# A list scheduler for the attention and gate stage of a fused transformer block, and the low part of the attention output taken from TensorE

## The chip, the cores and the metric

The kernel runs on one core of one Trainium2 chip. The metric is the device time of one execution in microseconds; lower is better. The core has five engines with a queue each: TensorE (PE, matmuls), VectorE (DVE), ScalarE (ACT), GpSimd (POOL) and SyncE (SP, which issues most DMAs). Each engine works off its own queue, in which its instructions stand in the program's order.

## The reference

`x` is the output of attention inside chunks of 64 rows (batch 8, 8 heads, 576 rows, head size 64). It goes through a gate, a projection and a feed-forward net:

```python
scores = scale * np.matmul(q_c, k_c.transpose(0, 1, 2, 4, 3))
scores = scores - np.max(scores, axis=-1, keepdims=True)
attn = np.exp(scores)
attn = attn / (np.sum(attn, axis=-1, keepdims=True) + 1e-09)
out = np.matmul(attn, v_c)
...
for k in range(K):
    gate_pre += conv_w[k][None, None, :] * xp[:, k:k + S, :]
gate = 1.0 / (1.0 + np.exp(-gate_pre))
val = x @ w_val
return (gate * val @ w_out).astype(np.float32)
...
ch = np.maximum(xn @ w_ch1, 0.0) @ w_ch2
return (x + ch).astype(np.float32)
```

The convolution has 5 taps, the model width is 512, the hidden width 2048, `xn` is a layer norm. Products keep float32 accuracy by splitting each operand into a high part (`F32R`) and a low part (operand minus high part): high·high, high·low and low·high are summed. The weights of the projections arrive as 64-bit numbers and are decoded on the chip to float32.

## The kernel before, in words

The 4608 rows of all batches are worked in 9 blocks of 512 rows (`NB`), and attention in 18 units of 256 rows (`NU`), two to a block.

For a unit u: `load_qkv` (line 78) fetches q, k and v. `a3` (line 152) makes the scores (S: 32 small matmuls, two records each in the trace), and the softmax on DVE in five steps (maximum line 167, subtract 170, sum 176, reciprocal 177, multiply 179) with the exponential on ACT (174). `a4` (181) turns the weights on PE (T: 8 transposes) and copies them out with ACT (pT, 188). `a5` (208) multiplies them with v (A: 32 small matmuls into the PSUM tile `x`, of which there is one) and takes three things out of PSUM: the float32 output `xf` (ACT, 233), its high part `xh` (ACT, 236) and its low part `xl` (DVE, 238: `x` minus `xh`).

For a block j: `conv` (243) computes the gate's sum in `cg`, the first tap on ACT (248), four more on DVE (250) for each of four column groups f, 16 operations of 128x516 to a block (in the first and last block 32 of 128x256 or a little more). `sigm` (255) is one sigmoid on ACT. `val` (266, called V here) is 12 matmuls of 512 columns for each f, into a PSUM ring `ps_d` of two buffers; its result is multiplied with the gate on DVE (`gv`, 282), and split by ACT (`gh`, 285) and DVE (`gl`, 286). A buffer of `ps_d` comes free with `gv`, which needs the sigmoid. `proj` (289, called O) is 12 matmuls for each of four row tiles, copied out by ACT (`y`, 299) and sent to DRAM. The multiplications of `chain` all have line 264.

The weights are decoded and split in between (`split`, 92): ACT (87), three DVE operations (88 to 90), ACT (95), and the low part on POOL (96). `early_ff` does so for the first 4 of 16 pairs of feed-forward weights.

What sets the order: `slot` (594) calls these functions by a table (`at`, lines 656 to 679). For the first four slots PE's order is the program's (`manual_schedule`); WARM adds dummy matmuls. From then on, and on all other engines throughout, the framework's scheduler sets the order by priority, which follows the program's order except under `high_priority`. After the last attention unit `prep` (623) starts the layer norm and the transposes (`turn_rows`, 343) for block 0 of the feed-forward stage, which then runs in its own order (lines 713 to 764) to the end.

Of the kernel before, what the change touches and what calls it, by code (L numbers as in the profile page):

```python
# [8 lines left out]
F32 = mybir.dt.float32  # L9
# [6 lines left out]
DRAM = bass.MemoryType.DRAM  # L16


@with_exitstack
def tile_chunk_attention_gated_mlp(ctx: ExitStack, tc: tile.TileContext, qk, v, w_val, conv_w, w_out, g_ln, w1, w2, out):  # L20
# [52 lines left out]
    gr = const.tile([CT, P], F32, name="gr")  # L73

# [23 lines left out]

    wv = {}

    def load_w(w, nm, slot0):
        raws = []
        for c in range(CT):
            raw = wA.tile([P, DM, 2], U32, tag=f"s{slot0 + c}", name="raw")
            nc.sync.dma_start(out=raw, in_=w[c * P:(c + 1) * P])
            raws.append(raw)
        wv[nm] = raws

    def split_w(nm, c0=0, c1=CT):
# [40 lines left out]
    pt, pT = {}, {}  # L150

    def a3(u):
        t = qkr.pop(u)
        kt, qt = t[:, 0], t[:, 1]
        sc = ps_s.tile([P, 2, NG, CH], F32, tag="sc", name="sc")
        for g in range(NG):
            n, hp = divmod(g, NP)
            for c in range(2):
                cs = slice(n * P + c * CH, n * P + (c + 1) * CH)
                for par in range(2):  # L160
                    r0 = CH * par
                    nc.tensor.matmul(
                        out=sc[CH * c:CH * c + CH, par, g, :], lhsT=qt[r0:r0 + CH, hp, cs], rhs=kt[r0:r0 + CH, hp, cs],
                        start=True, stop=True,
                    )
        mx = pA.tile([P, 2, NG], F32, tag="mx", name="mx")
        nc.vector.tensor_reduce(out=mx, in_=sc, op=ALU.max, axis=AX.X)  # L167
        whole = exps[u % len(exps)]
        ex = whole[:, :, :, 0:CH]
        nc.vector.tensor_tensor(  # L170
            out=ex.rearrange("p g r k -> p r g k"), in0=sc,
            in1=mx.unsqueeze(3).to_broadcast([P, 2, NG, CH]), op=ALU.subtract,
        )
        nc.scalar.activation(out=ex, in_=ex, func=ACTF.Exp, scale=scale)
        sm = pA.tile([P, NG, 2], F32, tag="sm", name="sm")
        nc.vector.tensor_reduce(out=sm, in_=whole, op=ALU.add, axis=AX.X)  # L176
        nc.vector.reciprocal(out=sm, in_=sm)
        pr = pt[u] = pA.tile([P, NG, 2, CH], F32, tag="pr", name="pr")
        nc.vector.tensor_tensor(out=pr, in0=ex, in1=sm.unsqueeze(3).to_broadcast([P, NG, 2, CH]), op=ALU.mult)

    def a4(u):
        pr = pt.pop(u)
        t = pA.tile([P, NG, P], F32, tag="pT", name="pT", bufs=1)
        ps = ps_p.tile([P, NG, P], F32, tag="p", name="pst")
        for g in range(NG):
            nc.tensor.transpose(out=ps[:, g, :], in_=pr[:, g].rearrange("p r k -> p (r k)"), identity=ident)
        with tc.high_priority():
            nc.scalar.activation(out=t, in_=ps, func=ACTF.Copy)
            pT[u] = t

    xf, xh, xl = {}, {}, {}

    def new_block(j):
        o = boundary(j)
        t = pD2.tile([P, CT, BLK + 2 * HALO], F32, tag="xf", name="xf")
        if j == 0:
            nc.gpsimd.memset(t[:, :, 0:HALO], 0.0)
        else:
            ob = boundary(j - 1)
            e = BLK + (HALO if ob < BLK else 0)  # L200
            nc.gpsimd.tensor_copy(out=t[:, :, 0:HALO], in_=xf[j - 1][:, :, e:e + HALO])
        if o < BLK:
            nc.gpsimd.memset(t[:, :, HALO + o:2 * HALO + o], 0.0)
        xf[j] = t
        xh[j] = pD2.tile([P, CT, BLK], F32R, tag="xh", name="xh")
        xl[j] = pD2.tile([P, CT, BLK], F32R, tag="xl", name="xl")

    def a5(u):
        t = pT.pop(u)
        j, uu = divmod(u, UPB)  # L210
        va = vr.pop(u)
        x = ps_x.tile([P, 2, NP // 2, UN], F32, tag="x", name="x")
        for i in range(NP // 2):
            for c in range(NC):
                n, cs = c // 2, slice(c % 2 * CH, (c % 2 + 1) * CH)
                for f in range(2):
                    for r in range(2):
                        r0, o0 = CH * r, CH * f
# [582 lines left out]
```

## Time and profile before

| what | us |
|---|---|
| median of 3 runs (1138.92 to 1139.91) | 1139.91 |
| span of the profiled execution, first to last instruction | 1134.2 |
| PE busy in the span | 1070.5 (94%) |
| DVE busy | 712.8 (63%) |
| ACT busy | 483.5 (43%) |
| POOL busy | 110.6 (10%) |

For the profiled execution its span is given and no total of its own; the median of the runs lies 5.7 us above the span. The span falls into three parts: the stage that is changed, from 0 to about 344 us, where the first feed-forward matmul starts; a first feed-forward block to about 456; and the rest, in which PE has hardly a gap. Two notes on reading: a row with "x64" merges that many instructions, and the durations of neighbours on one engine overlap a little, so that the step from one start to the next is the price of an instruction in a queue.

### The profile page before, as it was taken

Reading aid. Unit: us, or ns where it says so; the run is one execution under the profiler, and the core shown is the slowest. Engines: PE = TensorE matmul, PEld = TensorE weight load, DVE = VectorE, ACT = ScalarE, POOL = GpSimd, SP = SyncE. Lnnn points to the kernel's source line nnn. Section 1 sums busy time; section 2 is a strip of 40 time slices with the busy share of each in tenths; the row PEclk is TensorE's granted clock in tenths of the full one; section 3 lists DMA queues with packets and bytes.
Section 4 is the critical chain, followed back from the end, with each engine's and each line's share of the span. In section 5 each row is a group of like instructions: output and inputs, shape, how many; then the busy total and the mean of one; then the engine's idle time right before and its main releaser. Section 6 shows DMA issues by size and latency. Waiting matters only on the chain.

```text
span 1134.2 us, 17091 instructions
## 1 busy us (share of the span) xinstructions
PE 1070.5 (94%) x6862; PEld 871.4 (77%) x6862; DVE 712.8 (63%) x1171; ACT 483.5 (43%) x832; POOL 110.6 (10%) x120
## 2 busy tenths in 40 slices
PE   5788989899898989899999999999999999999998
PEld 5676767777786868688888888888888888878877
DVE  6999999888967877545647434447444437432434
ACT  3566666566574754434444123333223333221221
POOL 2021001000003443322210000000000000000000
PEclk9799999999999999999999999999999999999999
DMA  8535546531135753634342733332733222622212
GB/s 334 169 121 166 187 133 213 179 107 72 46 120 188 225 165 119 236 118 145 126 141 100 232 99 106 112 106 89 232 105 103 99 93 89 227 93 93 75 38 75
DMA packets 58581, 155.28 MB, mean 137 GB/s; under 512 B 5742, under 2 KB 13958, under 8 KB 56198
## 3 DMA queue, kind: packets, MB, share of 16 engines
q1 hardware_dynamic: 53318, 144.75, 37.7%
q10 hardware_dynamic: 5184, 9.44, 2.2%
q8 instruction: 54, 0.88, 0.3%
q14 instruction: 25, 0.20, 0.1%
HBM read 116.41 MB, written 37.75 MB: 136 GB/s over the span
## 4 chain that ended last, share of the span: by engine, by line
PE 65%; DVE 24%; issue 4%; ACT 3%; DMA 3%; POOL 0%; SPq 0%; ACTq 0%; POOLq 0%; DVEq 0%
PE acc L499 16%; PE x L525 15%; PE psf L499 14%; PE zy L525 10%; DVE cg L250 7%; PE psv L264 5%; DVE da L89 2%; DVE da L90 2%; DVE sm L176 2%; PE acc L385 1%; DVE xl L238 1%; DMA raw<-in_moe_w_ch 1%; DVE h L537 1%; PE psh L264 1%; DVE mx L167 1%
## 5 line engine op out<-in xcount | busy, mean ns | idle before, releaser
L545 DVE TENSOR_TENSOR c<-x,c 128x512 f32<-128x512 f32 x96 | 66.2, 690 | 237.3 <-ACT c L541 181.1
L499 PE MATMUL psf<-w,h 128*128 128x512 f32 x768 | 186.0, 391 | 0.0
L499 PE MATMUL acc<-w,h 128*128 128x512 f32 x768 | 186.0, 391 | 0.0
L499 PEld LDWEIGHTS acc<-w,h 128*128 128x128 f32 x768 | 144.2, 188 | 31.4
L499 PEld LDWEIGHTS psf<-w,h 128*128 128x128 f32 x768 | 144.2, 188 | 31.4
L525 PE MATMUL x<-t,wc 128*128 128x512 f32 x576 | 148.2, 393 | 3.4 <-DVE c L545 3.4
L541 ACT ACTIVATE c<-zy 128x512 f32<-128x512 f32 x96 | 58.0, 604 | 188.4 <-PE zy L525 188.3
L525 PEld LDWEIGHTS x<-t,wc 128*128 128x128 f32 x576 | 108.8, 189 | 27.8 <-DVE c L545 4.6
L536 ACT ACTIVATE h<-c 128x512 fp32r<-128x512 f32 x96 | 60.5, 631 | 136.1 <-DVE c L545 135.5
L250 DVE SCALAR_TENSOR_TENSOR cg<-xf,cw,cg 128x516 f32<-128x516 f32 (+1 forms) x176 | 108.6, 661 | 0.0
L504 DVE TENSOR_TENSOR yt<-psf,yt 128x512 f32<-128x512 f32 x128 | 88.2, 691 | 25.0 <-PE psf L499 21.1
L525 PE MATMUL zy<-b,wc 128*128 128x512 f32 x384 | 98.9, 393 | 0.0
L525 PEld LDWEIGHTS zy<-b,wc 128*128 128x128 f32 x384 | 71.2, 188 | 14.6
L537 DVE SCALAR_TENSOR_TENSOR h<-c,h 128x512 fp32r<-128x512 f32 x96 | 68.5, 713 | 14.0 <-ACT h L536 13.9
L264 PE MATMUL psv<-xh,vh 128*128 128x512 f32 x144 | 62.1, 432 | 15.5 <-DVE gv L282 15.5
L96 POOL TENSOR_TENSOR w<-da,w 128x512 fp32r<-128x512 f32 x32 | 48.6, 1526 | 128.8 <-ACT w L95 125.6
L264 PE MATMUL psv<-xh,vl 128*128 128x512 f32 x144 | 59.6, 414 | 0.0
L264 PE MATMUL psv<-xl,vh 128*128 128x512 f32 x144 | 59.6, 414 | 0.0
L264 PE MATMUL pso<-oh,gh 128*128 128x512 f32 x144 | 58.5, 406 | 0.1
L264 PE MATMUL pso<-oh,gl 128*128 128x512 f32 x144 | 56.5, 393 | 0.4 <-DVE gl L286 0.4
L264 PE MATMUL pso<-ol,gh 128*128 128x512 f32 x144 | 56.1, 390 | 0.0
L393 POOL TENSOR_TENSOR wc<-raws,wc 128x256 fp32r<-128x256 f32 x56 | 45.3, 831 | 107.4 <-ACT wc L392 100.5
(108 smaller groups left out, 1563.3 us busy)
## 6 DMA issues: line engine op xcount, KB each, us to landing
wc<-wc SPq DMA_DIRECT2D x112, 512.0 KB, 3.2
qkr<-in_qk SPq DMA_DIRECT2D x18, 1024.0 KB, 5.9
raw<-in_moe_w_ch SPq DMA_DIRECT2D x32, 512.0 KB, 4.2
vr<-in_v SPq DMA_DIRECT2D x18, 512.0 KB, 4.2
yd<-y ACTq DMA_DIRECT2D x36, 256.0 KB, 2.8
out<-yt SPq DMA_DIRECT2D x36, 256.0 KB, 3.7
yr<-yd SPq DMA_DIRECT2D x32, 256.0 KB, 3.2
yt<-yd SPq DMA_DIRECT2D x32, 256.0 KB, 4.1
```

Of the source, the lines that this page charges most:

```text
L89: nc.vector.scalar_tensor_tensor(out=au, in0=hw, scalar=0x80000000, in1=au, op0=ALU.bitwise_and, op1=ALU.bitwise_or)
L96: nc.gpsimd.tensor_tensor(out=lo, in0=a, in1=hi, op=ALU.subtract)
L250: nc.vector.scalar_tensor_tensor(out=o, in0=x[:, f, i + lo:i + hi], scalar=cw[:, i * CT + f:i * CT + f + 1], in1=o, op0=ALU.mult, op1=ALU.add,
L264: nc.tensor.matmul(out=ps, lhsT=lt, rhs=rh, start=(i == 0), stop=(i == n - 1))
L393: eng.tensor_tensor(out=lo, in0=a, in1=hi, op=ALU.subtract)
L499: nc.tensor.matmul(out=ps, lhsT=lt, rhs=rh, start=(g == 0 and k == 0 and (first or half)), stop=(g == 1 and k == 2 and (last or half)),)
L504: nc.vector.tensor_tensor(out=yt[i], in0=ps, in1=yt[i], op=ALU.add)
L525: nc.tensor.matmul(out=ps, lhsT=lt, rhs=rh, start=(start and c == 0 and i == 0), stop=(c == 1 and i == 2), skip_group_check=True)
L536: nc.scalar.activation(out=t[:, 0, :], in_=src, func=ACTF.Relu)
L537: nc.vector.scalar_tensor_tensor(out=t[:, 1, :], in0=src, scalar=0.0, in1=t[:, 0, :], op0=ALU.max, op1=ALU.subtract)
L541: nc.scalar.activation(out=t, in_=zy, func=ACTF.Copy)
L545: nc.vector.tensor_tensor(out=t, in0=x, in1=t, op=ALU.add)
```

## The change

It touches the first part alone. The functions `a3` to `proj` are taken apart into single steps, and each is handed to a `Plan` with its engine, an assumed cost, the steps that it comes after and a rank. `Plan.run` is a list scheduler in the kernel's Python: of all engines it takes the one that can start next, and on it the step of lowest rank among those that can start then. The instructions are then written in that order, and `manual_schedule` holds all five queues to it. What belongs to V, gate and O of the last block is put off (`late`) and written after `prep`, where the framework's scheduler orders it.

Besides:
- `xl` no longer comes from DVE. PE adds minus `xh` to the PSUM tile `x` (X: two matmuls of 512 columns with a negative unit matrix `minus` as weights), and ACT copies the difference out (`xl`). A, which summed nothing before, now clears with its first matmuls alone.
- the taps of column groups 0 and 1, and of 2 and 3, have ranks that make them alternate; V's and O's four sums are planned in quarters of three matmuls.
- the decoding of the feed-forward weights is 8 single halves, with a rank behind all else; dummy matmuls fill PE's planned gaps before the first V; `y` has three buffers in place of two; the framework's DMA scratch is smaller.

```diff
+    def run(self):
+        todo, users = {}, {n: [] for n in self.ops}
+        ready = {e: [] for e in self.starts}
+        free = dict(self.starts)
+        rings = {r: [0.0] * k for r, k in self.rings.items()}
...
+        while len(begun) < len(self.ops):
+            best = None
+            for e, waiting in ready.items():
+                at = {}
+                for t, n in waiting:
+                    ring = self.ops[n][6]
+                    if ring:
+                        if not rings[ring]:
+                            continue
+                        t = max(t, min(rings[ring]))
+                    at[n] = max(t, free[e])
+                if at:
+                    t = min(at.values())
+                    pick = min((self.ops[n][4], i, n) for i, n in enumerate(at) if at[n] <= t + 1e-9)[2]
+                    if best is None or t < best[0]:
+                        best = t, e, pick
+            t, e, n = best
+            _, cost, _, _, _, tail, take, give = self.ops[n]
+            ready[e] = [w for w in ready[e] if w[1] != n]
+            if take:
+                rings[take].remove(min(rings[take]))
+            begun[n], free[e], done[n] = t, t + cost, t + cost + tail
+            if give:
+                rings[give].append(done[n] + self.WAKE)
+            for m in users[n]:
+                todo[m] -= 1
+                if not todo[m]:
+                    ready[self.ops[m][0]].append((max(done[d] for d in self.ops[m][3]) + self.WAKE, m))
+        return sorted(begun.items(), key=lambda x: x[1])
...
-    LAG = 1
-    MANUAL = 4
     NC = UN // CH
...
-    WARM = {(0, 0): 2, (0, 1): 12, (0, 3): 12, (1, 1): 12, (1, 3): 12, (2, 1): 8, (2, 3): 12}
...
-            for lo, hi, sh in segs:
-                dst = xf[j][:, :, lo + sh:hi + sh].rearrange("p (r i) t -> p r i t", r=2)
-                nc.scalar.activation(out=dst, in_=x[:, :, :, lo - a:hi - a], func=ACTF.Copy)
-            for lo, hi, sh in segs:
-                dst = xh[j][:, :, lo:hi].rearrange("p (r i) t -> p r i t", r=2)
-                nc.scalar.activation(out=dst, in_=x[:, :, :, lo - a:hi - a], func=ACTF.Copy)
-                low = xl[j][:, :, lo:hi].rearrange("p (r i) t -> p r i t", r=2)
-                nc.vector.tensor_tensor(out=low, in0=x[:, :, :, lo - a:hi - a], in1=dst, op=ALU.subtract)
...
+    plan = Plan({"d": 2}, {"PE": 2.0, "DVE": 2.0, "ACT": 2.0, "POOL": 2.0, "SP": 0.7})
...
+        for c in range(CT):
+            raw("v", w_val, c, 0, -195 + c)
+        plan.add(("raw", "taps"), "SP", 1.5, taps, [("ld", 1)], -145, tail=4.0)
...
+            raw("o", w_out, c, CT, -90 + c)
+        for i in range(2 * NFA):
+            plan.add(("raw", "f", i), "SP", 0.6, lambda i=i: load_half(i), ([("dL", ("f", i - 2))] if i > 1 else [("dL", ("taps",))]) + [("S", 4 + i)], 50 * i, tail=5.0)
...
+        def subtract():
+            for r in range(2):
+                nc.tensor.matmul(
+                    out=t["x"][:, r], lhsT=minus, rhs=xh[j][:, 2 * r:2 * r + 2, a:b],
+                    start=False, stop=True, skip_group_check=True,
+                )
+
+        def low():
+            nc.scalar.activation(out=xl[j][:, :, a:b].rearrange("p (r i) t -> p r i t", r=2), in_=t["x"], func=ACTF.Copy)
+
+        soft = base - 150
+        plan.add(("S", u), "PE", 1.25, scores, [("ld", u)] + [("sub", u - 1)] * (u > 0), soft, tail=0.1)
+        plan.add(("mx", u), "DVE", dve(full), top, [("S", u)], soft)
+        plan.add(("sub", u), "DVE", dve(full), less, [("mx", u)] + [("mul", u - 2)] * (u > 1), soft)
+        plan.add(("exp", u), "ACT", act(full), lambda: nc.scalar.activation(out=ex, in_=ex, func=ACTF.Exp, scale=scale), [("sub", u)], soft)
+        plan.add(("sum", u), "DVE", dve(full + 16), total, [("exp", u)], soft)
+        plan.add(("rc", u), "DVE", 0.16, lambda: nc.vector.reciprocal(out=t["sm"], in_=t["sm"]), [("sum", u)], soft)
+        plan.add(("mul", u), "DVE", dve(full), weights, [("rc", u)] + [("T", u - 2)] * (u > 1), soft)
+        plan.add(("T", u), "PE", 0.87, turn, [("mul", u), ("pT", u - 1) if u else ("tC",)], soft + 10, tail=0.12)
+        plan.add(("pT", u), "ACT", act(full), turned, [("T", u)] + [("A", u - 1)] * (u > 0), soft + 10)
+        plan.add(("A", u), "PE", 1.25, values, [("pT", u)] + [("xl", u - 1)] * (u > 0), soft + 10, tail=0.2)
+        before = []
+        if j > 1:
+            before = [("V", j - 2, f, CT - 1) for f in range(CT)] + [("conv", j - 2, f) for f in range(CT)]
+        if uu == 0:
+            plan.add(("new", j), "POOL", 0.6, new_block, before + [("xf", u - 1)] * (j > 0), soft)
+        plan.add(("xh", u), "ACT", act(full), high, [("A", u), ("new", j)], soft + 20)
+        plan.add(("xf", u), "ACT", act(full) + 0.1 * (len(segs) - 1), both, [("xh", u)], soft + 25)
+        plan.add(("X", u), "PE", 0.46, subtract, [("xh", u), ("xf", u)], soft + 25, tail=0.17)
+        plan.add(("xl", u), "ACT", act(full), low, [("X", u)], soft + 30)
...
+                plan.add(name, "DVE", dve(hi - lo), lambda i=i: tap(i), [last] + ([("conv0", j, f)] if name[0] == "conv" and h else []), base + f // 2 + 0.1 * i)
...
+    nc.scalar.activation(out=minus, in_=ident, func=ACTF.Copy, scale=-1.0)
...
+    late, busy, dense = [], 1.0, False
+    with tc.manual_schedule(engines={mybir.EngineType.PE, mybir.EngineType.DVE, mybir.EngineType.Activation, mybir.EngineType.Pool, mybir.EngineType.SP}):
+        for name, at in plan.run():
+            engine, cost, fn = plan.ops[name][:3]
+            if name[0] in ("V", "gv", "gh", "gl", "O", "y") and name[1] == NB - 1:
+                late.append(fn)
+                continue
+            if engine == "PE":
+                dense = dense or name[0] == "V"
+                if not dense:
+                    warm(at - busy)
+                busy = at + cost
+            fn()
+    prep()
+    for fn in late:
+        fn()
```

The queues show what moved. First DVE, at the last full blocks: the operations between the multiplication of one block with its gate (gv) and the taps (cg) of the next. Of before:

```order
L176 TENSOR_REDUCE sm<-ex_143 128x16
L286 TENSOR_TENSOR gl<-gv,gh 128x512 x2
L177 RECIPROCAL sm<-sm 128x16
L179 TENSOR_TENSOR pr<-ex_143,sm 128x1024
L238 TENSOR_TENSOR xl<-x,xh 128x4x128
L250 SCALAR_TENSOR_TENSOR cg<-xf,cw,cg 128x516 x3
L238 TENSOR_TENSOR xl<-x,xh 128x4x128
L250 SCALAR_TENSOR_TENSOR cg<-xf,cw,cg 128x516 x4
L167 TENSOR_REDUCE mx<-sc 128x16
L250 SCALAR_TENSOR_TENSOR cg<-xf,cw,cg 128x516
L170 TENSOR_TENSOR ex_144<-sc,mx 128x2x8x64
```

and of the change:

```order
L509 TENSOR_TENSOR gv<-psv,cg 128x384
L509 TENSOR_TENSOR gv<-psv,cg 128x128
L509 TENSOR_TENSOR gv<-psv,cg 128x384
L509 TENSOR_TENSOR gv<-psv,cg 128x128
L357 TENSOR_REDUCE sm<-ex_144 128x16
L517 TENSOR_TENSOR gl<-gv,gh 128x512 x2
L429 RECIPROCAL sm<-sm 128x16
L360 TENSOR_TENSOR pr<-ex_144,sm 128x1024
L461 SCALAR_TENSOR_TENSOR cg<-xf,cw,cg 128x516 x16
L347 TENSOR_REDUCE mx<-sc 128x16
L350 TENSOR_TENSOR ex_145<-sc,mx 128x2x8x64
```

The `xl` operations (L238; a unit's in two pieces where a batch ends inside it) are gone, the 16 taps stand in one run, and after it the next unit's maximum and subtraction (mx, ex) come before the next gv.

Next SP, at the start: qkr and vr are a unit's q, k and v, the raw tiles the weights, cwu the taps' weights. Of before:

```order
L80 DMA qkr<-in_qk 128x2048
L82 DMA vr<-in_v 128x1024
L105 DMA raw<-in_moe_w_val 128x1024 x4
L80 DMA qkr<-in_qk 128x2048
L82 DMA vr<-in_v 128x1024
L583 DMA cwu<-in_moe_conv_w 20x256
L584 DMA gr<-in_moe_g_ln 4x128
L80 DMA qkr<-in_qk 128x2048
L82 DMA vr<-in_v 128x1024
```

and of the change:

```order
L133 DMA qkr<-in_qk 128x2048
L135 DMA vr<-in_v 128x1024
L254 DMA raw<-in_moe_w_val 128x1024 x4
L133 DMA qkr<-in_qk 128x2048
L135 DMA vr<-in_v 128x1024
L254 DMA raw<-in_moe_w_out 128x1024 x4
L133 DMA qkr<-in_qk 128x2048
L135 DMA vr<-in_v 128x1024
L259 DMA cwu<-in_moe_conv_w 20x256
L260 DMA gr<-in_moe_g_ln 4x128
```

The four loads of w_out now stand ahead of the third unit's and of the taps' weights.

Last DVE at the stage's end: the last block's gate (gv, gl) and the low part of the feed-forward input (xn), which hangs on all 16 copies xt. Of before:

```order
L286 TENSOR_TENSOR gl<-gv,gh 128x512 x2
L282 TENSOR_TENSOR gv<-psv,cg 128x512
L286 TENSOR_TENSOR gl<-gv,gh 128x512
L282 TENSOR_TENSOR gv<-psv,cg 128x512
L286 TENSOR_TENSOR gl<-gv,gh 128x512
L393 TENSOR_TENSOR xn_3520<-xt,xn_3519 128x4x256 x2
L88 TENSOR_SCALAR da<-da 128x512
L89 SCALAR_TENSOR_TENSOR da<-raw_3887,da 128x512
```

and of the change:

```order
L461 SCALAR_TENSOR_TENSOR cg<-xf,cw,cg 128x256 x4
L509 TENSOR_TENSOR gv<-psv,cg 128x512 x2
L636 TENSOR_TENSOR xn_3594<-xt,xn_3593 128x4x256 x2
L517 TENSOR_TENSOR gl<-gv,gh 128x512 x2
L509 TENSOR_TENSOR gv<-psv,cg 128x512 x2
L517 TENSOR_TENSOR gl<-gv,gh 128x512 x2
```

The low part xn was behind all four gl; it now stands ahead of the first. On ACT the high parts xn likewise stand ahead of all four gh.

## Rows read from the trace of the kernel before

**Rows 1.** Stretches: us, busy us of PE, PEld, DVE, ACT, POOL, clock, DMA, GB/s.

```profile
56.00:320.00 264.00, 238.16 (x2747) 191.25 (x2744) 243.29 (x379) 165.69 (x219) 21.31 (x24) 0.96 0.41 138
...
346.00:456.00 110.00, 101.89 (x439) 81.24 (x437) 88.48 (x152) 63.34 (x130) 47.26 (x36) 0.97 0.52 168
```

**Rows 2.** Waits of PE, 56 to 346 us: us in total, times, longest.

```profile
PE psv L264 <- DVE gv L282: 15.5, 6, 5.1
PE x L219 <- ACT pT L188: 9.5, 4, 3.2
```

**Rows 3.** The value chains' tile: ns min/median/max, first and last start.

```profile
L264 PE MATMUL psv<-xh,vh x144: 387/389/793, 56.0 to 331.5; 128*128 128x512 f32 x144
```

**Rows 4.** Three pieces of the chain that ended last: start, us, what.

```profile
253.69 2.66 DVE cg L250 x4
...
309.44 11.11 PE pso L264 x48
320.55 7.26 PE psv L264 x32
```

**Rows 5.** One steady block, and the first 20 us; columns of the first group.

```profile
0.00:20.00 20.00, 14.38 (x204) 13.55 (x204) 10.79 (x15) 7.03 (x10) 3.43 (x12) 1.00 0.93 365
237.29:270.14 32.85, 30.64 (x368) 24.63 (x368) 27.78 (x41) 19.66 (x26) 0.70 (x1) 0.95 0.35 124
```

**Rows 6.** Timeline of DVE in that block: start, us, operation, [idle before].

```profile
237.29 1.42 DVE L282 TENSOR_TENSOR gv<-psv,cg 128x320 f32<-128x320 f32 x4 [1.99 <-ACT cg L257]
...
257.41 0.74 DVE L250 SCALAR_TENSOR_TENSOR cg<-xf,cw,cg 128x516 f32<-128x516 f32 x1
258.07 1.21 DVE L170 TENSOR_TENSOR ex<-sc,mx 128x1024 f32<-128x1024 f32 x1
...
266.27 1.22 DVE L238 TENSOR_TENSOR xl<-x,xh 128x1024 fp32r<-128x1024 f32 x1
...
270.14 1.42 DVE L282 TENSOR_TENSOR gv<-psv,cg 128x384 f32<-128x384 f32 x4 [2.00 <-ACT cg L257]
```

**Rows 7.** Timeline of PE: an attention step among the long matmuls.

```profile
85.39 1.04 PE L186 MATMUL pst<-ident,pr 128*128 128x128 f32 x8
86.18 0.48 PE L264 MATMUL pso<-oh,gh 128*128 128x512 f32 x1
...
89.09 1.16 PE L219 MATMUL x<-pT,vr 64*64 64x64 f32 x64
90.18 0.50 PE L264 MATMUL psv<-xh,vh 128*128 128x512 f32 x1
90.52 0.39 PE L264 MATMUL psv<-xl,vh 128*128 128x512 f32 x1
```

**Rows 8.** By line and form, 0 to 345 us: busy us, mean ns, idle before.

```profile
L90 DVE SCALAR_TENSOR_TENSOR da<-raw,da 128x512 uint32<-128x512 uint32 x19 | 13.6, 713 | 0.1
...
L87 ACT ACTIVATE da<-raw 128x512 f32<-128x512 f32 x19 | 12.7, 673 | 16.1 <-DMA raw<-in_moe_w_val 7.5 <-DMA raw<-in_moe_w_ch 6.0 <-POOL vl L96 1.4
...
L233 ACT ACTIVATE xf<-x 128x1024 f32<-128x1024 f32 x12 | 12.3, 1022 | 6.5 <-PE x L219 5.7 <-ACT y L299 0.8
...
L88 DVE TENSOR_SCALAR da<-da 128x512 uint32<-128x512 uint32 x19 | 7.6, 411 | 10.2 <-ACT da L87 10.0
```

**Rows 9.** Timeline of ACT at the end of the stage.

```profile
318.85 1.28 ACT L331 ACT_TABLE_LOAD   x1 [0.39 <-ACT y L299]
320.15 0.21 ACT L331 ACTIVATE r<-ve 128x4 f32<-128x4 f32 x1
...
333.66 2.16 ACT L350 ACTIVATE xt<-pst,cw 128x128 f32<-128x128 f32 x8
335.66 1.11 ACT L392 ACTIVATE xn<-xt 128x1024 fp32r<-128x1024 f32 x1
```

**Rows 10.** Timeline of the start: DVE's first decode, first taps.

```profile
9.04 0.43 DVE L88 TENSOR_SCALAR da<-da 128x512 uint32<-128x512 uint32 x1 [9.04 <-ACT da L87]
...
35.58 7.44 DVE L250 SCALAR_TENSOR_TENSOR cg<-xf,cw,cg 128x256 f32<-128x256 f32 x16
```

More of the change, by code (lines that the diff above doesn't have):

```diff
@@ L16, with __init__, add @@
 DRAM = bass.MemoryType.DRAM
+class Plan:
+    WAKE = 0.06
+    def __init__(self, rings, starts):
+        self.ops, self.rings, self.starts = {}, rings, starts
+    def add(self, name, engine, cost, fn, after=(), rank=0.0, tail=0.08, take=None, give=None):
+        assert name not in self.ops, name
+        self.ops[name] = (engine, cost, fn, list(after), rank, tail, take, give)
+    def run(self):
[3 more added lines that the diff above has]
+        rings = {r: [0.0] * k for r, k in self.rings.items()}
+        begun, done = {}, {}
+        for n, op in self.ops.items():
+            todo[n] = len(op[3])
+            for d in op[3]:
+                users[d].append(n)
+            if not op[3]:
+                ready[op[0]].append((0.0, n))
+        while len(begun) < len(self.ops):
[27 more added lines that the diff above has]
+        return sorted(begun.items(), key=lambda x: x[1])
 @with_exitstack
@@ L73, in tile_chunk_attention_gated_mlp @@
     gr = const.tile([CT, P], F32, name="gr")
+    minus = const.tile([P, P], F32R, name="minus")
     qkr, vr = {}, {}
@@ L149, in tile_chunk_attention_gated_mlp @@
         nc.gpsimd.memset(t[:, :, :, CH:CH + 1], 1e-9)
[L150 to L206, printed above, removed]
@@ L678, in tile_chunk_attention_gated_mlp @@
-    for f in range(NFA):
-        at(NU + LAG - 2 + f // 2, 1 + 2 * (f % 2), lambda f=f: early_ff(f))
-    head = ExitStack()
-    head.enter_context(tc.manual_schedule(engines={mybir.EngineType.PE}))
-    for u in range(NU + LAG + 4):
-        if u == MANUAL:
-            head.close()
-        slot(u)
-        if u == NU + LAG - 1:
-            with tc.high_priority():
-                sigm(NB - 1)
-            prep()
+    plan_loads()
+    plan_weights()
+    for u in range(NU):
+        plan_attention(u)
@@ new lines, in tile_chunk_attention_gated_mlp, with warm @@
+    for j in range(NB):
+        plan_block(j)
+    def warm(idle):
+        n = min(int((idle - 0.3) / 0.25), 28)
+        if n > 2:
+            ps = ps_d.tile([P, BLK], F32, tag="d", name="psw")
+            for _ in range(n):
+                nc.tensor.matmul(out=ps[:, 0:P], lhsT=ident, rhs=ident, start=True, stop=True)
+    late, busy, dense = [], 1.0, False
[11 more added lines that the diff above has]
+            fn()
```

412 lines of the change are left out of this document (258 added, 154 removed).

## The prediction

> **What bounds the kernel now.** I read the stretches first, then PE's waits, then one block of the middle on DVE and on PE. In the stage that is changed PE is busy 238 of 264 us and DVE 243 of 264, at a mean granted clock of 0.96, so that part of PE's busy time is at the lower of its two levels, 1.2 GHz [rows 1]. PE's named waits there are 15.5 us for gv, which frees a buffer of `ps_d`, and 9.5 us for pT [rows 2]. V of block 0 starts at 56.0 [rows 3], V of the last block at 320.55 [rows 4]: eight blocks in 264.5 us, 33.07 each. Which engine sets this period is seen in one block, from gv to gv: of 32.85 us DVE works 27.78 [rows 5], and of its 5.1 us without work 2.0 lie in one piece ahead of gv, where it waits for the sigmoid after its own last tap [rows 6]. PE's contents are less. A matmul of 512 columns costs 11.11/48 = 0.231 us [rows 4], so V and O of a block cost 96 x 0.231 = 22.2. A costs 1.09 and T 0.79, by the starts [rows 7], and S has the same 64 records as A: 2 x 2.97 = 5.9 for the two units. That is 28.1 in a period of 33.07. So DVE, together with the ring taps, sigmoid, gv, V, sets the pace, and PE waits about 5 us a block, part of it as slower clock.
>
> **The change, part by part.**
>
> *xl off DVE.* Two operations of 128x1024 a block at 1.22, less an overlap of 0.08 with the neighbour: 2.3 us. DVE's contents go from 27.78 to 25.5.
>
> *X onto PE.* Four matmuls of 512 columns, 4 x 0.231 = 0.93. The first long matmul after another kind takes 0.34 to the next start instead of 0.23 [rows 7], four such places more a block: 0.44. PE's contents go from 28.1 to 29.5, and PE becomes the engine with the most work in a block.
>
> *xl onto ACT.* No row has this copy; the nearest is xf, same shape and source, 1.02 [rows 8]. ACT's busy time in a block goes from 19.66 [rows 5] to 21.7. In the blocks that also decode two weight halves, two ACT operations each of some 0.65 (0.67 in [rows 8] for the first) make it 24.3. I cost this at nothing: it stays below PE's 29.5. What hides it is a queue with 5 us to spare; if that cover is gone, rival C.
>
> *Alternating taps.* Worth nothing. A tap alone between other work has a step of 0.66 (257.41 to 258.07 [rows 6]), and four in a run take 2.66, 0.665 each [rows 4]. If dependent taps lost anything now, runs would be dearer than single ones. At most 0.06 each (0.665 against 0.605, what 512 columns of other operations would leave), 112 taps, 6.7 us, lies between this and zero; DVE is no longer the bound, so I take zero.
>
> *One order for five queues.* The sigmoid's 2 us on DVE are now filled: maximum and subtraction of the next unit stand there. So the period can fall towards PE's 29.5, but not to it: with DVE at 25.5 (and 3.7 more, two halves of three operations, 0.41 + 0.71 + 0.71 each [rows 8], in the early blocks) two nearly full queues must mesh, and gv of columns 2 and 3 still waits for V. Bounds: 29.5 if PE never waits; 31.5 if DVE sets the pace, its 27.78 - 2.3 plus the 5.1 us of gaps it has now, and about 1 for the decodes. I take 30.2, nearer the low end, since the wait of 2.0 is the one that the new order visibly fills. Eight blocks: 8 x (33.07 - 30.2) = **-22.9**.
>
> *The start.* DVE's first decode is at 9.04, and V starts at 56.0. Before, 16 taps of block 0 (7.44 [rows 10]) and two xl (2.4) stood on DVE ahead of the third unit's softmax, on which V's start hangs; now they don't: -9.8. Against it, the taps' weights now stand behind 8.5 MB of loads instead of 5; at 365 GB/s [rows 5] they land at 23.3 instead of 13.7, and ACT's decode of them stands ahead of the second unit's exponential in ACT's queue. DVE is there at about 20.3 (9.04, six operations of 1.14, two decodes of 1.83, 0.7 of small ones): +3.0. Each unit's way from A to the next A gets an X and a hand-over more, about 0.65, twice: +1.3. Sum **-5.5**, between -10 and 0.
>
> *The end of the stage.* The last block's gl now stand behind xn on DVE and gh behind xn on ACT, while PE's last O needs gl. From PE's last transpose: half a group of eight xt, 1.1; two xn on ACT, 2.1 [rows 9]; the second xn on DVE, 1.2 (as the 128x1024 operations of [rows 6]); gl 0.6; hand-overs 0.5; together 5.5, of which five matmuls of V cover 1.1. PE stands still for **+4.4**, between 0 (if V runs late) and 8 (if the clock falls as well). The matmuls behind it are O of this block, then the feed-forward stage, whose inputs are ready in both kernels.
>
> *Nothing:* `minus` (one small ACT operation under the first loads), `y`'s third buffer, the scratch size, and the loads on SP past the start. The decodes that the feed-forward stage leans on are as many before the stage's end as now, to within one half; its 110 us [rows 1] I leave as they are, give or take 3.
>
> Sum: -22.9 - 5.5 + 4.4 = -24.0 on a span of 1134.2, so 1110.2. The median of the runs lies 5.7 above that span, which gives **1116**.
>
> **ACT's tables, by row and by rule.** Each block switches ACT's table twice, sigmoid and exponential. In the trace a load takes 1.28 with 0.39 idle ahead of it, and the next operation starts 0.02 after it [rows 9]: 1.7 a switch. The Trainium skill ("ScalarE: Activation LUTs", section "What ACT_TABLE_LOAD costs") states about 2.66 us for every switch, a drain of 1.38 included, and advises against alternating table sets, which is what this order keeps doing. By that rule ACT's early blocks would come to an estimated 24.3 + 2 x 1.0 = 26.3, and rival C would gain weight. The row shows less, and my sum goes by the row.
>
> **The rivals.**
> - A: PE full. 29.5 a block (-28.6), the start as above, only 2 lost at the end: -32, 1108. For it: DVE's and ACT's contents are both below PE's. Against: a buffer ring of two.
> - B: DVE remains the pace. 31.5 a block (-12.6), -5.5, +4.4: -13.7, 1126. For it: decodes in the first five blocks, and each tap costs 0.06 more than its width says, so a plan that counts by width runs late.
> - C: ACT's queue binds where decodes lie in it. No gain in the first four blocks: -11.5 - 5.5 + 4.4 = -12.6, 1127. For it: sigmoid, xl and exponential stand in one queue, and a late tap holds all three. Against: 5 us of slack.
> - D, the other side: the waits on PE stay as they are, because fixed queues hand a late sigmoid on to xl and so to A, and the added PE work is paid in full: 8 x 1.37 = 11.0, and 4.4 at the end, with no earlier start: +15.4, 1155. It decides once PE's waits exceed 3.6 a block, 33.07 less 29.5. Against: 2.0 of the present waits is one gap with an obvious filler, and DVE, on which PE waits, gets 2.3 less to do.
> - E: the change does not do what it says. For the taps I expect that; if the queues changed nothing else, removing xl alone would leave about 1126, as in B.
>
> **How the numbers follow.** Forecast 0.45, A 0.20, B with E 0.20, C 0.05, D 0.06, no change 0.04. A measurement of this kernel tells 0.2% from no change, 2.3 us. All but the last two and a remnant of C are faster: 0.88; same 0.04; slower 0.08. The range reaches below A by the start's bound (-5) to 1103, and above C by the end's bound and the feed-forward stage's 3 to 1134; D lies outside.
>
> **What would show it.** The profile after should have V of block 0 at about 50, block periods of about 30.2, PE's wait for gv well under 15 us, no L238-like operation on DVE, taps at 0.66 as now, a gap of some 4 us on PE ahead of the last O, and the first feed-forward matmul at about 320. I am wrong if the periods stay above 32, if V starts after 56, or if the feed-forward stage changes by more than 3.

## The result, and the profile after

The changed kernel takes 1122.98 us (median of 4 runs, 1119.83 to 1125.13) against 1139.91 (1138.92 to 1140.28): a ratio of 0.9856, 95% interval 0.9832 to 0.9880. The forecast was 1116 in 1103 to 1134. The profiled execution took 1121.67, its span 1119.9, 14.3 less than before. The medians differ by more, 16.9: in this execution the time is 1.8 above the span, so the profiled execution of the kernel before, with a span of 1134.2, took an estimated 1136.0, some 3.9 under its median. What follows accounts for the 14.3. Of the executions counted further down one, of the kernel with the halves' low parts on VectorE, was slow, at 2140.84 us; it is in that kernel's median and not in its ratio.

The same four stretches of both kernels show where they came from: first V matmul to the second half of V of block 0, from there to V of block 7, from there to the first feed-forward matmul, and the feed-forward stage to the first matmul of the last loop. Columns as in [rows 1]. The kernel before:

```profile
56.00:70.23 14.23, 11.44 (x222) 9.30 (x219) 14.01 (x24) 8.48 (x11) 1.64 (x2) 0.90 0.43 146
70.23:292.70 222.47, 202.50 (x2359) 162.17 (x2359) 204.00 (x302) 140.87 (x186) 19.68 (x22) 0.95 0.44 144
292.70:344.01 51.31, 48.23 (x284) 39.70 (x281) 36.99 (x79) 33.31 (x56) 0.00 (x0) 1.00 0.30 106
344.01:445.70 101.69, 93.94 (x405) 75.01 (x404) 82.62 (x141) 60.67 (x122) 42.78 (x31) 0.97 0.52 167
```

and the changed one:

```profile
52.41:69.73 17.32, 10.45 (x169) 8.44 (x163) 16.50 (x33) 9.99 (x12) 1.54 (x1) 0.87 0.45 155
69.73:279.75 210.02, 203.23 (x2449) 163.83 (x2445) 187.46 (x286) 154.00 (x194) 20.90 (x22) 0.99 0.44 155
279.75:334.28 54.53, 49.85 (x288) 39.18 (x282) 33.60 (x74) 35.02 (x58) 0.00 (x0) 1.00 0.29 106
334.28:432.00 97.72, 91.92 (x403) 74.08 (x404) 83.86 (x141) 60.79 (x122) 41.80 (x31) 0.98 0.56 181
```

V starts 3.6 earlier, but its second half only 0.5 (70.23 to 69.73). The blocks give 12.5, the end of the stage takes 3.2 back, the feed-forward stage is 4.0 shorter, and 0.6 lies in the last loop, which the change does not touch. DVE, busy 92% of the blocks before, is now at 89%, and PE at 97% (203.23 of 210.02) where it was at 91%, with the clock at 0.99 instead of 0.95. PE's time without work there falls from 20.0 to 6.8; its busy time stays (202.50 and 203.23) though X has come in, since more of it is at full clock.

PE's waits from 52 to 346 us, against [rows 2]:

```profile
PE sc L340 <- issue: 6.8, 1, 6.8
PE psv L499 <- ACT y L539: 4.3, 1, 4.3
PE pso L532 <- ACT gh L513: 2.5, 1, 2.5
PE pso L532 <- DVE gv L509: 1.7, 2, 1.3
PE pst L369 <- DVE pr L360: 1.4, 1, 1.4
PE x L384 <- ACT pT L373: 0.8, 2, 0.4
```

Of the many waits for gv and pT 1.7 and 0.8 us are left. Three single ones hold most of the rest. A period runs from V of one block to V of the next, so the first starts with V of block 0 and the sixth with V of the sixth block. The third to the seventh period:

```profile
122.59:151.76 29.17, 29.17 (x372) 23.74 (x370) 27.06 (x43) 21.72 (x28) 3.81 (x4) 1.00 0.49 173
151.76:181.22 29.46, 29.46 (x378) 24.31 (x372) 28.30 (x48) 22.59 (x28) 3.73 (x4) 1.00 0.40 142
181.22:213.10 31.88, 30.21 (x379) 24.14 (x373) 28.68 (x44) 22.81 (x30) 4.54 (x4) 1.00 0.61 215
213.10:249.35 36.25, 31.79 (x378) 25.00 (x373) 30.99 (x47) 23.47 (x29) 3.35 (x3) 0.95 0.50 177
249.35:279.75 30.40, 30.33 (x381) 24.70 (x375) 24.74 (x39) 23.47 (x28) 1.15 (x1) 1.00 0.17 60
```

PE is full in the first two, and the period there is what its contents are. The fifth period, 31.88, has a wait of 1.3 for gv. The sixth, 36.25, has the one of 4.3 for y, and PE's busy time is longer in it, 31.79 at a clock of 0.95: it is some 6.4 over the 29.8 at which PE is full in a later run. The cause of the 4.3 is seen on ACT, just after 213:

```profile
209.87 0.62 ACT L236 ACTIVATE w<-da 128x512 fp32r<-128x512 f32 x1
210.39 0.59 ACT L539 ACTIVATE y<-pso 128x512 f32<-128x512 f32 x1
...
216.24 0.69 ACT L140 ACTIVATE da<-raw 128x512 f32<-128x512 f32 x1 [5.26 <-POOL w L240]
...
217.74 0.57 ACT L539 ACTIVATE y<-pso 128x512 f32<-128x512 f32 x1
```

ACT's next decode waits 5.26 for a GpSimd subtraction that frees its buffer. Behind it in ACT's queue stands the copy of y, which frees a buffer of `ps_d` for V of the sixth block: PE's 4.3. The GpSimd operation and VectorE beside it:

```profile
188.68 1.30 POOL L240 TENSOR_TENSOR w<-da,w 128x512 fp32r<-128x512 f32 x1 [19.36 <-ACT w L236]
...
210.57 5.64 POOL L240 TENSOR_TENSOR w<-da,w 128x512 fp32r<-128x512 f32 x1 [7.73 <-ACT w L236]
```

```profile
203.99 10.76 DVE L461 SCALAR_TENSOR_TENSOR cg<-xf,cw,cg 128x516 f32<-128x516 f32 x16 [1.25 <-ACT cg L458]
214.66 0.43 DVE L141 TENSOR_SCALAR da<-da 128x512 uint32<-128x512 uint32 x1
215.00 1.23 DVE L347 TENSOR_REDUCE mx<-sc 128x16 f32<-128x1024 f32 x1
```

The subtraction takes 1.3 us where it runs freely, as at 188.68; here it takes 5.64 and ends 1.2 after the maximum, the first operation after 16 taps in a row that reads PSUM, begins. The planner has it at 1.4.

### The profile page after: what moved, and what is told of

Read it like the earlier page. It is cut to its first block, busy times and chain, and to the rows that moved or that the text cites. A ratio compares the mean times of both kernels' runs of the same rounds, so it can differ in the third digit from the quotient of the medians.

```text
span 1119.9 us, 17199 instructions
## 1 busy us (share of the span) xinstructions
PE 1074.1 (96%) x6928; PEld 874.7 (78%) x6928; DVE 688.5 (61%) x1147; ACT 501.1 (45%) x846; POOL 112.7 (10%) x120
## 4 chain that ended last, share of the span: by engine, by line
PE 75%; DVE 12%; ACT 5%; issue 3%; DMA 3%; POOL 1%; SPq 0%; ACTq 0%; POOLq 0%
PE acc L742 16%; PE x L768 15%; PE psf L742 15%; PE zy L768 10%; PE psv L499 6%; PE pso L532 6%; PE acc L628 1%; DVE da L142 1%; DVE h L780 1%; PE psh L197 1%; DMA qkr<-in_qk 1%; PE sc L340 1%; PE pst L591 1%; DVE cg L461 1%; DVE da L143 1%
## 5 line engine op out<-in xcount | busy, mean ns | idle before, releaser
L461 DVE SCALAR_TENSOR_TENSOR cg<-xf,cw,cg 128x516 f32<-128x516 f32 (+1 forms) x176 | 104.0, 656 | 1.7 <-ACT cg L458 1.6
L499 PE MATMUL psv<-xh,vh 128*128 128x512 f32 x144 | 59.1, 411 | 4.3 <-ACT y L539 4.3
L499 PE MATMUL psv<-xl,vh 128*128 128x512 f32 x144 | 57.3, 398 | 0.0
L499 PE MATMUL psv<-xh,vl 128*128 128x512 f32 x144 | 57.0, 396 | 0.0
L779 ACT ACTIVATE h<-x 128x512 fp32r<-128x512 f32 x32 | 19.2, 600 | 81.1 <-PE x L768 81.1
```

The costliest lines, as they stand in the source:

```text
L461: nc.vector.scalar_tensor_tensor(out=out, in0=xf[j][:, f, i + lo:i + hi], scalar=cw[:, i * CT + f:i * CT + f + 1], in1=out, op0=ALU.mult, ...
L499: nc.tensor.matmul(out=x["v", f], lhsT=lt[:, fs], rhs=rh[j][:, c, :], start=(c == 0 and k == 0), stop=(c == CT - 1 and k == 2))
L779: nc.scalar.activation(out=t[:, 0, :], in_=src, func=ACTF.Relu)
```

## The experiments

Each kernel was timed in five rounds (one in three) against the kernel before on the same chip; ratios and 95% intervals are to that kernel. In the text "the base" is the changed kernel. Edits are shown shortened, with ... for what is left out.

**The base again.** No edit.

> The changed kernel once more, unaltered, as the base for what follows. Theory 1 (one long hold-up): between the fifth and sixth block ACT stands still some 5 us for one GpSimd subtraction that lasts 5.6 instead of 1.3 us while VectorE works through 16 taps in a row, and PE then waits 4.3 us for ACT's copy of y; the order of the queues is fixed, so this comes again at the same place, 4 to 6 us long, and the time is 1120 to 1125. Theory 2 (chance): the hold-up belongs to that one execution; it is somewhere else or gone, and with it 4 to 6 us.

1123.14 us, 0.9868 (0.9848 to 0.9888). V of the sixth block waits 4.36 for y, in the same place; the GpSimd subtraction takes 5.70. Theory 1: the hold-up belongs to the order, not to one execution.

**xl back on VectorE, order kept.**

```
-nc.scalar.activation(out=xl[j][...], in_=t["x"], func=ACTF.Copy)
+nc.vector.tensor_tensor(out=lo, in0=t["x"], in1=hi, op=ALU.subtract)
-plan.add(("X", u), "PE", ...)
-plan.add(("xl", u), "ACT", act(full), low, [("X", u)], soft + 30)
+plan.add(("xl", u), "DVE", dve(full), low, [("xh", u), ("xf", u)], soft + 30)
```

> xl goes back to VectorE inside the same planner: no X matmuls on PE, no xl copy on ACT. If the gain comes from the order of the five queues (PE sets the pace): PE has 1.4 us less in a block, and the time is between 1112 and 1125. If it comes from VectorE's relief (VectorE sets the pace, and 2.4 us a block more come back on it): 1130 to 1140. I expect between the two, 1128, nearer the second, since VectorE was busy 92% of the attention stage before.

1119.11 us, 0.9827 (0.9806 to 0.9848). My 1128 was wrong: the time falls in the range for the order. The change without X gives no less than the whole of it, and X adds nothing to the planned order. Two blocks of this kernel:

```profile
184.10:214.40 30.30, 28.89 (x370) 23.36 (x368) 29.83 (x45) 20.45 (x27) 1.49 (x3) 1.00 0.45 152
214.40:245.70 31.30, 28.78 (x373) 23.59 (x369) 30.37 (x47) 20.53 (x26) 1.48 (x3) 1.00 0.44 161
```

Now DVE is full (29.83 of 30.30), and PE has 1.4 to spare. There is no hold-up on ACT here.

**X on TensorE, the old order kept.** In the kernel before, X stands in PE's order behind the first chain that follows A; the copy xl has high priority, xh is one operation a unit, and the framework's DMA scratch is the smaller one of the changed kernel.

```
-nc.vector.tensor_tensor(out=low, in0=x[...], in1=dst, op=ALU.subtract)
+nc.tensor.matmul(out=x[:, r], lhsT=minus, rhs=xh[j][:, 2 * r:2 * r + 2, a:b], start=False, ...)
+nc.scalar.activation(out=xl[j][...], in_=x, func=ACTF.Copy)
-        for fn in d[2] + d[3]:
+        for fn in d[2] + [X and xl of this unit] + d[3]:
```

> The kernel before, in its old order, with xl from TensorE: two X matmuls a unit in PE's order, put behind the first chain that follows A, and xl a copy on ACT. If VectorE's contents set the old pace, 2.4 us less on VectorE a block, at 1.4 us more on PE: 8 to 12 us less than before, about 1129, with a period of some 31.8. If what sets it is the chain of taps, sigmoid, gv and V whatever VectorE holds besides: periods stay at 33 and the time within 3 us of before, or longer by up to 11 where PE's new work is paid. The changed kernel with xl back on VectorE came out faster than with X, so I expect little: -3 us.

1115.57 us, 0.9791 (0.9774 to 0.9809): 24 us less than before, eight times what I expected, and faster than the base, whose interval lies above. The second, third, fifth and sixth period, and the rest from V of block 7 to the feed-forward stage:

```profile
90.60:126.60 36.00, 32.20 (x381) 25.21 (x373) 35.15 (x54) 25.93 (x34) 4.79 (x5) 0.95 0.51 176
126.60:159.80 33.20, 30.23 (x378) 24.18 (x373) 32.92 (x52) 25.40 (x33) 4.82 (x5) 1.00 0.66 223
...
190.90:220.70 29.80, 29.80 (x376) 24.18 (x372) 26.21 (x40) 21.15 (x26) 0.80 (x2) 1.00 0.43 143
220.70:250.50 29.80, 29.80 (x379) 24.22 (x372) 25.79 (x39) 21.16 (x26) 0.80 (x2) 1.00 0.42 142
...
280.40:329.30 48.90, 48.90 (x288) 39.99 (x285) 32.97 (x74) 35.25 (x58) 0.00 (x0) 1.00 0.32 113
```

Where nothing is decoded PE is full, in the old order as well: 29.80 of 29.80. The planned order can give little there (its own full blocks take 29.17 and 29.46). It saves in the early blocks (30.7, 29.2 and 29.5 against 36.0, 33.2 and 31.1) and loses that again: 6.4 in the sixth period with the hold-up, 2.1 in the fifth, 5.6 at the end (54.53 against 48.90), and 5.6 in the first block (39.45 against 33.80), which gives back an earlier start. The feed-forward stage, which X does not touch, is shorter here as well, 98.7 (329.34 to 428.0) against 101.7 before; whether the smaller scratch has a part in that was not run.

**A fourth buffer for the decodes**, so that a decode on ACT waits for the low part four back; matmul for matmul the same order on PE. The other tiles of that tag, those of the feed-forward stage among them, get four buffers too.

```
-before = [("lo", decoded[k - 3])] if k > 2 else []
+before = [("lo", decoded[k - 4])] if k > 3 else []
-a = tiles["da", key] = stg.tile(..., tag="da", bufs=3)
+a = tiles["da", key] = stg.tile(..., tag="da", bufs=4)
```

> A fourth buffer for the decoded weights, so that ACT's next decode waits for the GpSimd subtraction before the last one, not for the last; PE's order stays the same, matmul for matmul. Theory 1 (hold-up of ACT behind GpSimd): PE's wait of 4.3 us before V of the sixth block goes, and the slower clock after it: 4 to 6 us less than the changed kernel, about 1118; the 16 taps in a row still stretch the GpSimd operation to 5 us or more, only nobody waits. Rival (ACT or VectorE is simply full, and PE's wait is only where their lateness shows): the wait moves elsewhere, and the time stays within 1.5 us.

The fifth and the sixth period, and the feed-forward stage:

```profile
180.10:212.40 32.30, 30.21 (x381) 24.14 (x373) 29.14 (x45) 24.83 (x33) 4.57 (x4) 1.00 0.61 212
212.40:242.90 30.50, 30.19 (x377) 24.40 (x372) 30.36 (x46) 22.07 (x27) 2.97 (x3) 1.00 0.67 227
329.59:434.41 104.82, 95.75 (x405) 76.17 (x405) 82.32 (x141) 59.80 (x121) 41.79 (x32) 0.95 0.51 165
```

The period of 36.25 is 30.50, at full clock, though the subtraction still takes 5.27: it is ACT's wait for it that cost, 5.75 in this period, not its length. The fifth period stays, at 32.30, so its 2 us over PE's contents are not the hold-up. The time is 1123.75, 0.9867 (0.9852 to 0.9881), as the base, which is the rival's figure, but not by the rival's way: the wait did not move within the stage, and the feed-forward stage takes 104.82 instead of 97.72 and gives all of it back. That the four buffers do that there isn't shown.

**GpSimd out of these decodes, and the stage's end.** First the end alone:

```
 for name, fn in late:
+    if name[0] in ("gv", "gh", "gl"): with tc.high_priority(): fn()
```

> The last block's gv, gh and gl get high priority, so that gh and all but one gl stand ahead of the xn operations on ACT and VectorE. Theory (the stage's end costs 3.9 us because gh and gl stand behind xn): PE's gap of 2.5 us and the slow V matmuls ahead of the last projection go, 3 to 4 us less than the changed kernel, about 1119.5. Rival (the first feed-forward matmuls then wait for xn instead): within 1 us of the changed kernel.

1122.19, 0.9862 (0.9840 to 0.9884): not told from the base in time, so neither theory nor rival is decided by it. In the trace the 2.5 for gh becomes 0.5 for gl, and from V of block 7 to the first feed-forward matmul it takes 52.4 (279.5 to 331.94) instead of 54.53, 2.1 of the 3 to 4 expected; the next matmuls do not wait for xn. Then with the feed-forward halves' low parts on VectorE:

```
-nc.gpsimd.tensor_tensor(out=lo, in0=tiles["da", key], in1=hi, op=ALU.subtract)
+(nc.vector if key[0] == "f" else nc.gpsimd).tensor_tensor(out=lo, ...)
-plan.add(("lo", key), "POOL", 1.4, low, [("hi", key)], rank)
+plan.add(("lo", key), *(("DVE", dve(width)) if key[0] == "f" else ("POOL", 1.4)), low, ...)
```

> The changed kernel, with the low parts of the feed-forward weight halves subtracted on VectorE in place of GpSimd (the planner puts them in its order with VectorE's cost), and the last block's gv, gh and gl at high priority. Theory 1 (the changed kernel loses some 6 us to ACT held up behind a stretched GpSimd operation and some 3 to the stage's end, and is otherwise paced by PE): the hold-up between the fifth and sixth block is gone with the GpSimd operation, the blocks from the third to the eighth take 29 to 31 us each, the first feed-forward matmul starts at 325 to 329, and, since the feed-forward stage's buffers are left as they are, its length stays at 98: 1113 to 1117, level with the old order with X. Rival (a planned order is rigid, and each block has some late wait whichever is cured): 1119 to 1125.

1116.43, 0.9809 (0.9781 to 0.9836), inside the expected 1113 to 1117. The sixth period is 29.5, the first feed-forward matmul starts at 324.58, just ahead of the expected 325. Two parts were missed: the feed-forward stage is 101.3, not 98, and the fourth period is 34.05, not 29 to 31, as VectorE, with the low parts on it, is full there:

```profile
152.95:187.00 34.05, 33.37 (x504) 26.59 (x503) 33.98 (x53) 27.51 (x32) 0.24 (x2) 1.00 0.45 151
```

The sum fits the reading that the hold-up and the end are what the base loses against X in the old order. It is no proof of it, since the new order shifts other periods as well.

> xl back on VectorE inside the planner, and the last block's gv, gh and gl at high priority. With xl on VectorE the gap ahead of the last projection was 1.3 us and the stage's end otherwise as long: 1 to 3 us less than the 1119 without the priority, 1117; no more, as its blocks are paced at 30.3 by VectorE.

(The two earlier edits together.) 1115.08 in three rounds, 0.9790 (0.9759 to 0.9821), as expected within 2 us.

**The sigmoid's cost in the planner**: `act(CT * n) + 2.6` becomes `act(CT * n) + 0.2`.

> One number in the planner: the sigmoid costs 0.2 us over its width instead of 2.6 (in the trace ACT stands idle ahead of it and its table is already loaded, and it takes 1.93 in all). gv of block 0 then stands on VectorE ahead of the fifth unit's subtraction and the decode, not behind them. Theory (the start is paced by VectorE's work up to gv of block 0, and this misplaced gv costs 3 us of it): the second half of V of block 0 starts at about 66.5 instead of 69.7, 3 us less in all. Rival (the order that comes out is another one everywhere, with another luck in each block): the second half starts 3 us earlier, but the time differs by anything between -5 and +8.

V's second half in block 0 starts at 66.27, 3.5 earlier, as expected, though 1.3 of that is there at V's first matmul already (51.13). The time is 1131.95, 0.9937 (0.9924 to 0.9951), beyond the rival's bound. PE's waits from 70 us on:

```profile
PE psv L499 <- DVE gv L509: 5.4, 3, 2.9
PE psv L499 <- ACT y L539: 4.0, 4, 1.9
PE x L415 <- ACT xf L411: 2.2, 1, 2.2
```

A cost nearer to the trace gives a worse order: many small waits instead of one of 4.3. What in the planner turns it that way wasn't followed.

**Taps one after the other**: the rank `base + f // 2 + 0.1 * i` becomes `base + f + 0.1 * i`.

> The conv's taps no longer alternate between two of the four column groups: each chain of four taps is planned behind the last. If dependent taps lost anything, the mean of a 516-wide tap would rise from 0.67 by up to 0.06 us, 112 of them, up to 6.7 us of VectorE's time and some 2 to 6 us in all. My forecast said nothing: the tap's duration stays at 0.66 to 0.67, and the time stays within 3 us, either way, by the other order alone.

The taps of this kernel, mean in ns behind the bar:

```profile
L461 DVE SCALAR_TENSOR_TENSOR cg<-xf,cw,cg 128x516 f32<-128x516 f32 x112 | 77.7, 754 | 1.2 <-ACT cg L458 1.1
```

and of the base:

```profile
L461 DVE SCALAR_TENSOR_TENSOR cg<-xf,cw,cg 128x516 f32<-128x516 f32 x112 | 76.0, 749 | 1.6 <-ACT cg L458 1.6
```

Dependent taps cost nothing that shows. 1123.52, 0.9872 (0.9854 to 0.9891), the base's time, though no subtraction is stretched to 5 us in this order: after the first period the longest is now the fifth, 37.45 (184.57 to 222.02), and PE waits 4.2 for gh at the end. An order without that hold-up is not yet a faster one.

**One decode a block, in the old order with X**: each half's load waits for its block's attention output.

```
+nc.gpsimd.tensor_copy(out=t[:, 0, :].bitcast(F32), in_=xf[j][:, 0, BLK:BLK + 2])
 nc.sync.dma_start(out=t, ...)
-at(NU + LAG - 2 + f // 2, 1 + 2 * (f % 2), lambda f=f: early_ff(f))
+at(UPB * j + UPB, 3, lambda j=j: early_half(j))
```

> The old order with X on PE, and each of the eight feed-forward weight halves of this stage loaded only once the block it is assigned to (one half a block, first to eighth) has its attention output; before, all eight were decoded by 155 us. Theory (in the old order with X, blocks 2 to 4 take 36.0, 33.2 and 31.1 us in place of PE's 29.8 because two to three decodes a block fill VectorE to 97%): with one decode a block VectorE holds 28 of 29.8, these blocks come to 29.8 to 31, and 6 to 10 us go: about 1107. Rival (those blocks are long because the chain of taps, sigmoid and gv has not yet settled after the start, or because PE's clock is lower there): within 2 us of 1115.6, or longer, since the later blocks get a decode each.

1132.64, 0.9948 (0.9928 to 0.9967): my theory fell. Two periods and the wait:

```profile
123.20:157.20 34.00, 31.61 (x380) 25.36 (x373) 28.42 (x43) 22.13 (x28) 2.34 (x5) 0.95 0.43 140
...
257.10:289.10 32.00, 30.14 (x380) 24.20 (x372) 28.13 (x42) 22.82 (x29) 2.22 (x4) 1.00 0.29 95
```

```profile
PE psv L272 <- DVE gv L290: 11.4, 6, 2.4
```

DVE holds 28.4 of 34.0, so it isn't full, and yet each block waits for gv: one decode a block puts the last tap so late that sigmoid and gv are waited for again, as in the kernel before (in the last of these periods gv starts 8.5 after V; it is 5.4 in the sixth period of the old order with X, which has no decode). All decodes in three blocks harm three blocks; one in each harms all.

**X for every second unit**, with the end's priority, and the same with the low parts on VectorE.

```
+if uu: plan.add(("X", u), "PE", ...); plan.add(("xl", u), "ACT", ...)
+else:  plan.add(("xl", u), "DVE", dve(full), low, [("xh", u), ("xf", u)], soft + 30)
```

> Inside the planner, X for the second unit of each block alone and xl of the first on VectorE, with the last block's gv, gh and gl at high priority. Theory (with X for both, PE is the fuller engine: busy 259 of 270 us; with none, VectorE: 249 of 270; each sets its kernel's pace): at half, PE has some 256 and VectorE some 241, both have slack, and the time is 1109 to 1113, below the 1115 and 1116 of the two ends. Rival (both ends are paced by late waits of the fixed order, not by contents): 1113 to 1122, with waits at other places.

> The same, and the feed-forward halves' low parts on VectorE in place of GpSimd. Theory (contents set the pace, and a stretched GpSimd operation holds ACT only by chance of the order): VectorE gets 5 us more over the stage, PE stays the fuller: within 2 us of the kernel without this, unless that has a hold-up of 4 to 6 us behind a GpSimd operation, which then is gone here. Rival (the order decides): anything from 1111 to 1124, with no such hold-up to point at.

1119.36, 0.9845 (0.9825 to 0.9864), and 1113.99, 0.9788 (0.9765 to 0.9811). The first lies outside the theory's 1109 to 1113: both engines have room (251.8 and 238.4 of 270 us), and PE waits 3.4 and 3.3 at single places of the order. It has no stretched GpSimd operation in the late blocks, and yet a sixth period of 37.1 (210.95 to 248.08), so what the second gains over it is the order's doing too, as the rival has it. The second has the lowest median of all, level within the intervals with X in the old order, and faster than both kernels of this study.

## Why the prediction was right, and where it was not

**Direction and size.** Forecast 1116, measured 1123, in the range; the first feed-forward matmul came at 334.3, where I had about 320. That the total is as near as this is in part luck. Of the 24.0 forecast for the stage the trace shows 9.7; of the 16.9 measured, 4.0 lie in the feed-forward stage, 0.6 in the last loop, and 2.6 in which execution of each kernel was profiled, and for none of these had I a term. The cause named, PE's waits filled until PE sets the pace, is shown: the four periods without the start and the two long ones (30.73, 29.17, 29.46, 30.40) average 29.9 against the 30.2 taken, and PE's contents, forecast 29.5, are 29.80 in the old order with X. All seven average 32.5: the other three (39.45, 31.88, 36.25) stay near or above the 32 that I gave as a sign of being wrong.

**The start, -5.5, was a failed step.** V's first matmul came 3.6 earlier, but I collected the gain there. What PE waits for next is a score matmul and then gv of block 0, and both hang on VectorE. Up to gv of block 0 VectorE, the third busy time, has 6.0 us less to do (before, then changed):

```profile
0.00:69.48 69.48, 47.27 (x832) 42.42 (x832) 56.80 (x87) 31.43 (x44) 9.46 (x18) 0.85 0.63 232
0.00:67.62 67.62, 48.39 (x746) 43.80 (x746) 50.76 (x82) 33.52 (x46) 11.01 (x18) 0.91 0.63 235
```

It loses most of that to the taps' weights, whose late landing I had at +3.0. On ACT their decode waits for the load, and behind it VectorE stands idle for 6.4:

```profile
26.49 0.32 ACT L214 ACTIVATE da<-cwu 20x128 f32<-20x128 f32 x1 [10.39 <-DMA cwu<-in_moe_conv_w]
```

```profile
27.39 0.55 DVE L218 TENSOR_SCALAR da<-da 128x512 uint32<-128x512 uint32 x2 [6.41 <-ACT da L214]
```

Then comes the order ahead of gv:

```profile
64.75 1.22 DVE L347 TENSOR_REDUCE mx<-sc 128x16 f32<-128x1024 f32 x1
65.89 0.69 DVE L226 SCALAR_TENSOR_TENSOR da<-raw,da 128x512 uint32<-128x512 uint32 x1
66.49 1.22 DVE L350 TENSOR_TENSOR ex<-sc,mx 128x1024 f32<-128x1024 f32 x1
67.62 1.29 DVE L509 TENSOR_TENSOR gv<-psv,cg 128x512 f32<-128x512 f32 x2
```

The sigmoid ended at 64.65. The planner, which has it some 2.5 longer, put three operations ahead of gv. PE stands from 60.98 to 67.81 at a score matmul, which the profile calls "issue"; its start falls 0.1 after the subtraction above, which frees the scores' buffer, so I read it as a wait for that. After that gap the score matmuls take 1.99 instead of 1.16, and V's second half follows them. So 0.5 was gained, not 5.5 (0.8 in the base's second execution, 1.9 with the end's priority). With the sigmoid's cost changed in the planner, gv comes ahead of that subtraction and the second half comes 2.2 sooner after V's first matmul.

**The blocks, -22.9.** From V's second half in block 0 to V of block 7 it was -12.5; some 6.6 blocks at 2.87 would have been -18.9. The second to the seventh period sum to 187.9, 6.7 more than six of 30.2, and the sixth alone has 6.05 of that. The step that failed is "ACT: I cost this at nothing". Its contents did stay below PE's (23.5 of 36.25 in the period with the hold-up); what my sum of contents could not hold is one wait at the head of its queue, with y behind it. Rival C named the queue, but with a late tap at its head, and in the early blocks.

**The end, +4.4,** measured +3.2: right in place and cause, gh behind xn ([rows 9] had xn's price), as the run with priority shows: PE's waits there are 2.5 for gh and 0.3 for gl, and 2.1 went with it.

**The taps, 0:** right. **The feed-forward stage, 0 give or take 3:** -4.0, and -3.1 in the base's second execution (98.6, 335.97 to 434.6): beyond the 3, which was one of my signs of being wrong. It took 97.7 to 104.8 in the changed kernel and its variants, and 98.7 in the old order with X, which has the smaller scratch too: the planned order is not needed for the gain, and why the stage is shorter wasn't settled.

**Rivals.** E had it that xl off VectorE would give 1126 in the old order; it gives 1115.6, in blocks without decodes at rival A's pace of a full PE. B's pace, a full VectorE, came in the planned order without X (29.83 of 30.30), not with it. D, slower, did not come: the old waits did not stay. The dear table switches that would have helped C did not show: in the changed kernel xf ends at 219.74 and the sigmoid behind its load of 1.28 starts at 221.05, so a switch is 1.3. My 1.7 was read too high: of the 0.39 idle, 0.33 is ACT's issue of a DMA. Whether X's 11 us on PE are paid inside the planned order isn't shown: xl on VectorE is 0.9827 there and X 0.9868, but only the second has the hold-up, and with that and the end mended the two are level (1115.08 and 1116.43).

## What to carry to other kernels

Two parts of a change that draw on the same waits do not add: xl on TensorE alone gave 24 us, the planned order without it 19 to 20, both together 15 to 17. Run each alone before keeping both. And in fixed queues contents do not set the price of a step: one decode that waited 5.3 us at the head of ACT's queue cost some 6 in a period of which ACT was busy 23.5 of 36.25, so look at what each engine waits for in order, and collect a gain only at the last point that still waits for it.

## What the hardware showed

VectorE's taps, which read two operands from SBUF, and GpSimd's subtraction keep each other out, and either may be the one that waits. Before, the subtraction got into the first of these two runs of eight taps and lies outside the second:

```profile
150.15 6.45 DVE L250 SCALAR_TENSOR_TENSOR cg<-xf,cw,cg 128x516 f32<-128x516 f32 x8
...
185.34 5.41 DVE L250 SCALAR_TENSOR_TENSOR cg<-xf,cw,cg 128x516 f32<-128x516 f32 x8
```

```profile
152.49 1.56 POOL L96 TENSOR_TENSOR w<-da,w 128x512 fp32r<-128x512 f32 x1 [3.94 <-ACT w L95]
```

The first run takes 6.45, 1.04 more than the second, most of the subtraction's 1.3. In the changed kernel 16 taps ran unbroken at 0.67 and the subtraction waited: it took 5.64 and 5.70 in two executions, 5.10 with the end's priority and 5.27 with the fourth buffer, at the same place of the order. The Trainium skill ("SBUF — State Buffer", section "SBUF: two separate sides") says that the two engines share a pair of ports under an exclusive lock, also where the VectorE operation has two SBUF inputs, and that the one which comes second is blocked in full. Both rows agree with a full block. What no run here shows is why the lock went one way before and the other way now.
